# Block attention and two expert networks: scores of two heads in one visit on 64 rows each, late jobs staggered by one, products of the second network in another order

## Chip, cores and metric

The kernel runs on one core of a Trainium2 chip. The metric is the device time of one execution in microseconds (us); smaller is better. The time before is 913.89 us, the median of three runs (913.84 to 914.25).

## What is computed

Four sequences of 576 tokens go through attention with 8 heads of 64, with a mask by blocks of 64 tokens (a query sees its own block of keys and all earlier ones). The result, 2304 tokens by 512, goes through a network that takes the larger of three products, and then through a gated network:

```python
scores = scale * np.matmul(q, k.transpose(0, 1, 3, 2))      # (4, 8, 576, 576)
scores = np.where(block_i >= block_j, scores, -1e9)
attn = softmax(scores)
x = np.matmul(attn, v)                                       # then (2304, 512)
h = np.maximum(np.maximum(x @ w1, x @ w2), x @ w3)           # 512 -> 768
x = h @ w_out                                                # 768 -> 512
gate = 1.0 / (1.0 + np.exp(-(x @ w_gate)))                   # 512 -> 1536
out = (gate * (x @ w_val)) @ w_out2                          # 1536 -> 512
```

## The kernel before

The first part holds attention and the first network ("experts"), the second part the gated network. Most products are made in fp32r, a faster form of fp32 that keeps fewer bits; so an operand is split into a high part (rounded) and a low part (what is left), and a product becomes three: high by high, high by low, low by high. Value products and transposes stay in fp32.

**Jobs.** Attention is cut into 32 jobs. A job is a sequence and a pair of heads. Sixteen early jobs take the first 256 queries and keys (row blocks 0 and 1 of 128 queries), sixteen late jobs the other 320 queries (row blocks 2 and 3, and the 64 queries of block 4) with all 576 keys. A job loads keys, queries and values (`load_qk`, `load_v`), splits keys and queries (`high_q` and a copy make the high parts, `low_q` and a subtraction the low ones), and makes scores (`scores`, lines 383 and 384). Masking (`hide`), the largest score, the exponential with its sum (line 405) and the division (`norm`) follow on VectorE and ScalarE. The weights are transposed on TensorE (`turn`, line 458; block 4 in `turn_four`, line 474) and copied to the tile `PT` (`keep`, `keep_four`); `apply` (line 496) multiplies them by the values, one head on columns 0 to 63 of the array and one on 64 to 127. `split` then writes the high and low parts of the result for the experts.

**Scores before.** The queries' tile holds high parts in rows 0 to 63 and low parts in rows 64 to 127, the keys stand twice, once for each half. So two matmuls over 128 rows make all of one head's scores for a row block:

```python
T.matmul(s, j.qp[:, qc : qc + 128], KP[:, h, ck], start=True, stop=False)   # 383
T.matmul(s, j.qp[:, qc : qc + 128], KL[:, h, ck], start=False, stop=True)   # 384
```

Block 4 has 64 queries of each head. Both heads' queries stand side by side with zeros between, four matmuls of 288 columns for each half of the keys (`scores_four`, lines 425 and 426).

**Experts.** Chunks of 256 tokens (early) and 320 (late) go through `experts` (lines 529 to 531, twelve matmuls a step) and `project` (lines 574 to 576).

**Order.** TensorE has two streams: A is attention, M the experts. A table `visits` places the steps of attention (S0, S1 and S4 are scores, T0, T1 and T4 transposes, P the value products) between expert steps, with lengths `LEN`; numbers in `PLAN` set starts, gaps and due times. `plan` then goes through all operations in time, with a cost for each, and decides which engine's instruction comes next; every engine issues in that order, SP's DMAs as well. Besides, the weights of the gated network, which arrive in a 64-bit format, are converted, combined and parked in DRAM during the first part.

**Second part.** The gated network takes blocks of 768 tokens as two by two halves and makes four products of halves from seven (Winograd's form of Strassen's method). `product` issues one of the seven as six matmuls of 384 columns (lines 1207 to 1209), in three banks a, b and c for each of its twelve blocks of weights: 1 and 2 go to a, 6, 7 and 4 to b, 5 and 3 to c. `first`, `last` and `middle` set the order 1 6 5, then 3 and 4 of the previous one (written 3' 4'), then 2 7. Additions on VectorE (line 1220) and a copy on ScalarE (line 1291) read a bank before the next product adds into it. `take_w` loads weights, `out_unit` (lines 1261 to 1263) makes the output.

Of the kernel before, what the change touches and what calls it, by code (L numbers as in the profile page):

```python
# [8 lines left out]
F32 = mybir.dt.float32  # L9
# [25 lines left out]
QKN = 2 * S + 640  # L35
# [12 lines left out]
    "t0": 7.09,  # L48
    "gap0": 0.34,
    "wgap": -0.02,  # L50
    "tail": 3,
    "prep": 2.18,
    "soft": 4.73,
    "keep": 2.54,
    "xsplit": 4.81,
    "evac": 1.08,
    "hcast": 5.75,
    "convb": 50.0,
    "load": 22.63,
    "park0": 116.98,  # L60
    "park": 19.23,
    "parko": 8.0,
    "slack": 100.0,
    "spare": 0.29,
    "start": 79.92,
# [5 lines left out]
RING = {"qk": 2, "v": 4, "s": 3, "t": 2, "o": 1, "m": 2, "w": 8, "raw": 4, "tmp": 4, "st": 3}  # L71
# [3 lines left out]
def block_attention_moe_moe(ctx: ExitStack, tc, k1, q1, v1, k2, q2, vt, wa, wb, out):  # L75
# [55 lines left out]
    ps_o = att.enter_context(tc.tile_pool(name="ps_o", bufs=RING["o"], space=PSUM))  # L131

    ident = ap1.tile([128, 128], F32, name="ident")
    zero = ap1.tile([128, 64], F32, name="zero")
# [3 lines left out]
    QP = [ap1.tile([128, 704], F32R, name=f"Q{i}") for i in range(2)]  # L138
    KP = ap1.tile([128, 2, S], F32R, name="K")
    KL = ap1.tile([128, 2, S], F32R, name="L")  # L140
# [5 lines left out]
    PT = ap1.tile([128, 2, 1408], F32, name="PT")  # L146
    EO = [0, 128, 0, 384]
    SEG = {(0, 2): 0, (0, 3): 1, (1, 2): 2, (1, 3): 3, (2, 2): 4, (2, 3): 5, (3, 3): 6}
# [161 lines left out]
    def add_job(b, p, late):  # L310
        j = Job()
        j.b, j.p, j.late = b, p, late
        j.i = len(jobs)
        j.tiles = (2, 3) if late else (0, 1)
        alt = not late and p % 2
        j.k0 = 288 if alt else 0
        j.nkc = S if late else 256
        j.nq = 320 if late else 256
        j.eo = 448 if alt else 0
        j.qp = QP[j.i % 2]  # L320
        j.qt = [0, 448] if late else [0, 256]
        jobs.append(j)
# [9 lines left out]
    def load_qk(j):  # L332
        n = 2 * j.nkc
        if j.i < 3:

            j.raw = first[:, 1024 * j.i : 1024 * j.i + 1024]
# [15 lines left out]
    def kcols(j, n=None):  # L352
        return slice(j.k0, j.k0 + (n or j.nkc))

    def high_q(j):
        if j.late:
            for h in range(2):
                A.activation(j.qp[0:64, 384 * h : 384 * h + 320], j.qr[:, h], AF.Copy, scale=SCALE)
        else:
            A.activation(j.qp[0:64, :512], j.qr.rearrange("p h n -> p (h n)"), AF.Copy, scale=SCALE)  # L360

    def low_q(j):
        def f(o, i, hi):
            V.scalar_tensor_tensor(out=o, in0=i, scalar=SCALE, in1=f32(hi), op0=ALU.mult, op1=ALU.subtract)

        if j.late:
            for h in range(2):
                c = slice(384 * h, 384 * h + 320)
                f(j.qp[64:128, c], j.qr[:, h], j.qp[0:64, c])
        else:  # L370
            f(j.qp[64:128, :512], j.qr.rearrange("p h n -> p (h n)"), j.qp[0:64, :512])

    def scores(j, h, i):

        ps = ps_s.tile([128, 512], F32, tag="s", name="ps_s")
        j.bank[h, i] = ps
        ts = (j.tiles[i],) if j.late else j.tiles
        for t in ts:
            s = ps[:, : 128 * (t + 1)] if j.late else ps[:, 128 * t : 128 * t + 128 * (t + 1)]
            j.s[h, t] = s  # L380
            qc = j.qt[h] + 128 * (t - j.tiles[0])
            ck = kcols(j, 128 * (t + 1))
            T.matmul(s, j.qp[:, qc : qc + 128], KP[:, h, ck], start=True, stop=False)  # L383
            T.matmul(s, j.qp[:, qc : qc + 128], KL[:, h, ck], start=False, stop=True)  # L384

# [12 lines left out]
    def largest_score(j, h, i):  # L398
        c = 2 * h + i
        V.tensor_reduce(out=j.nm[:, c : c + 1], in_=j.s[h, j.tiles[i]], axis=AX.X, op=ALU.max, negate=True)  # L400

    def expo(j, h, i):
        t, c = j.tiles[i], 2 * h + i
# [11 lines left out]
    def norm(j, h, i, e):  # L415
        t, c = j.tiles[i], 2 * h + i
# [3 lines left out]
    def scores_four(j, i):  # L420
# [40 lines left out]
    def keep(j, h, g, e):  # L461
        ps, n = j.tp[h, g[0]], len(g)
        if j.late:
            o = 192 * SEG[g[0]]
            d = PT[:, h, o : o + 192 * n].rearrange("p (s c) -> p s c", c=192)[:, :, :128]
            copy(e, d, ps[:, : 128 * n].rearrange("p (s c) -> p s c", c=128))
# [10 lines left out]
    def keep_four(j, i, e):  # L477
        if i == 0:
            d = PT[:, :, :1152].rearrange("p h (k s) -> p k h s", k=3)[:, :, :, 128:192]
            copy(e, d, j.tp4[0][:, 0:3])  # L480
        elif i == 1:
            copy(e, PT[:, :, 192 * 5 + 128 : 192 * 6], j.tp4[0][:, 3])
        else:
            copy(e, PT[0:64, :, 192 * 6 + 128 : 192 * 7], j.tp4[1][0:64, 0])

    def apply(j):


        j.o = ps_o.tile([128, 512], F32, tag="o", name="ps_o")
        if j.late:  # L490
            parts = [(0, 0, 320), (384, 0, 320), (768, 0, 320), (1088, 128, 192), (1280, 128, 64)]
# [133 lines left out]
    for j in jobs:  # L625
        p = jobs[j.i - 1] if j.i else None
        if not j.late:
            visits += [[(j, "S0"), (j, "S1")], [(p, "T0"), (p, "T1")] if p else [], [(p, "P")] if p else []]
        else:
            v = [[(j, "S0")], [(j, "S4")], [(j, "S1")], [(j, "T0")], [(j, "T4")], [(j, "T1")]]  # L630
            v[1].append((p, "P"))
            if not p.late:
                v[0] = [(p, "T0"), (p, "T1")] + v[0]
            visits += v
    visits += [[], [(jobs[-1], "P")]]
    LEN = {"S0": (0.47, 0.82), "S1": (0.47, 0.82), "S4": (0, 1.06), "T0": (0.35, 0.77),
           "T1": (0.35, 0.77), "T4": (0, 0.5), "P": (0.95, 2.5)}
# [41 lines left out]
    def build():  # L679
        z = Op("V", 0.6, lambda: (V.memset(zero, 0.0), V.memset(PT[64:128, :, 1280:1344], 0.0)), [])  # L680
# [176 lines left out]
        def job(j):  # L857
# [3 lines left out]
            ring = "qk" if i >= 3 else None  # L861
            ld = Op("S", 0.2, lambda: load_qk(j), [], ring=ring, size=384e3 if not j.late else 752e3)
            lv = Op("S", 0.1, lambda: load_v(j), [], ring="v", size=128e3 if not j.late else 320e3)
            kold = after(*[S_ops[x] for x in range(max(0, i - 2), i) if x in S_ops and (j.late or x == i - 2)])
            qold = S_ops.get(i - 2, [])
            n = j.nkc * 2
            kh = Op(*both(n, False), lambda e: copy(e, KP[:, :, kcols(j)], j.kr), [ld] + kold)
            zq = []
            if j.late and i < 4 * B + 2:
                zq = [Op("V", 0.15, lambda: V.tensor_copy(j.qp[:, 320:384], zero), qold + [z])]  # L870
            qh = Op("A", 0.56 if not j.late else 0.8, lambda: high_q(j), [ld] + qold)
            kl = Op(*vec(n), lambda: sub("V", KL[:, :, kcols(j)], j.kr, f32(KP[:, :, kcols(j)])), [kh])
            ql = Op("V", 0.61 if not j.late else 0.84, lambda: low_q(j), [qh])
# [3 lines left out]
            prep = [kl, ql] + zq  # L877
# [3 lines left out]
            N = {0: [], 1: []}  # L881
            eold = [j2 for j2 in (jobs[i - back],)] if i >= back else []
# [3 lines left out]
            Tn = {}  # L886
            RC = []

            def softmax(h, s, k, head):
# [3 lines left out]
                x = Op(*act(n, 1), lambda: expo(j, h, k), after([r], *[e.t_ops[h] for e in eold]))  # L893
                r.late = x.late = pos(f"S{h}") + P["soft"]
                s.frees.append(x)
                X[h].append(x)

            for h in range(2):
                for k in range(2) if j.late else (0,):
                    c = (0.36, 0.465)[k] if j.late else 0.46  # L900
                    s = pe("A", c, lambda h=h, k=k: scores(j, h, k), prep, pos(f"S{h}") + 0.1 * k, ring="s")
                    S_ops[i].append(s)
                    d = [s]
                    hd = Op("V", 0.11 if j.late else 0.13, lambda h=h, k=k: (small(j) if h == 0 and k == 0 else None, hide(j, h, k)), d + ([first_hide] if (h, k) != (0, 0) else []))
                    if (h, k) == (0, 0):
                        first_hide = hd
                    hd.late = pos(f"S{h}") + P["soft"]
                    for kk in ((k,) if j.late else (0, 1)):
                        softmax(h, s, kk, hd)
                if j.late and h == 0:  # L910
# [494 lines left out]
```

## Time and profile before

| | |
|---|---|
| median of three runs | 913.89 us |
| the profiled execution's own time | 915.82 us |
| its span | 914.0 us |
| TensorE busy | 887.0 us (97%) |
| VectorE busy | 597.8 us (65%) |
| ScalarE busy | 487.5 us (53%) |
| chain of waits, TensorE's share | 86% |
| granted TensorE clock over the span | 0.996 |

A busy share is an average over the whole span, and the engines have different shares in different stages; so the windows by stage are needed beside it. Matmuls overlap each other, so the distance from one start to the next tells what one costs, and not its duration. A record of the trace may be half of an instruction: value products are ten instructions with 320, 192 and 64 columns and twenty records.

### The profile page before, as it was taken

What the parts mean: (1) busy time and instruction counts of PE and PEld (TensorE: products, weight loads), DVE (VectorE), ACT (ScalarE), POOL (GpSimd) and SP (SyncE); (2) the same over time, 40 slices, a digit from 0 to 9 for tenths busy, and PEclk for the clock granted to TensorE, in tenths of its full rate; (3) what the DMA queues carried; (4) which work ended last, traced back from release to release, by engine and by line L of the source; (5) the groups of instructions that cost most, each with busy time, mean ns of one, the idle gap of its engine ahead of it and who ended that gap; (6) DMA issues with size and microseconds to landing.
All of it is one profiled execution on the core that took longest, in us unless ns stands there. A gap on an engine that the chain in (4) does not pass through costs nothing.

```text
span 914.0 us, 15702 instructions
## 1 busy us (share of the span) xinstructions
PE 887.0 (97%) x5696; PEld 826.0 (90%) x5696; DVE 597.8 (65%) x1372; ACT 487.5 (53%) x1098; POOL 96.6 (11%) x91
## 2 busy tenths in 40 slices
PE   5799999999999999999999998999999999999997
PEld 4689999999989989998999898888999988999986
DVE  7999958789899799788643876851455630455400
ACT  6889435457567566467422664631666621566311
POOL 0000000000000000000001553400132300132300
PEclk9899999999999999999999999999999999999999
DMA  9942345524655645643534988863789743779232
GB/s 314 374 121 63 99 143 174 182 75 154 209 165 191 199 148 174 189 137 104 188 119 143 310 249 259 279 213 132 247 251 320 238 130 129 251 259 310 78 104 80
DMA packets 85885, 171.42 MB, mean 188 GB/s; under 512 B 11312, under 2 KB 24624, under 8 KB 85808
## 3 DMA queue, kind: packets, MB, share of 16 engines
q1 hardware_dynamic: 85808, 170.43, 57.5%
q8 instruction: 44, 0.72, 0.3%
q14 instruction: 33, 0.27, 0.1%
HBM read 132.64 MB, written 37.75 MB: 186 GB/s over the span
## 4 chain that ended last, share of the span: by engine, by line
PE 86%; DVE 7%; DMA 3%; ACT 2%; issue 1%; SPq 0%; ACTq 0%; DVEq 0%
PE acc L1207 8%; PE acc L1209 8%; PE acc L1208 8%; PE ps_m L529 8%; PE ps_m L531 7%; PE ps_m L530 7%; PE acc L1262 5%; PE acc L1263 5%; PE acc L1261 5%; PE ps_o L496 5%; PE ps_t L458 3%; PE ps_m L574 3%; PE ps_m L576 3%; PE ps_m L575 3%; PE ps_s L383 2%; PE ps_s L384 2%
## 5 line engine op out<-in xcount | busy, mean ns | idle before, releaser
L529 PE MATMUL ps_m<-XT,w 128*128 128x256 f32 (+1 forms) x576 | 176.0, 305 | 1.6 <-ACT m L538 0.6
L530 PE MATMUL ps_m<-XT,w 128*128 128x256 f32 (+1 forms) x576 | 170.4, 296 | 0.8 <-DVE XT L98 0.8
L531 PE MATMUL ps_m<-XT,w 128*128 128x256 f32 (+1 forms) x576 | 170.6, 296 | 0.4 <-DVE w L98 0.3
L529 PEld LDWEIGHTS ps_m<-XT,w 128*128 128x128 f32 x576 | 109.0, 189 | 5.3 <-ACT m L538 1.1
L530 PEld LDWEIGHTS ps_m<-XT,w 128*128 128x128 f32 x576 | 109.2, 190 | 1.9 <-DVE XT L98 1.0
L531 PEld LDWEIGHTS ps_m<-XT,w 128*128 128x128 f32 x576 | 109.0, 189 | 0.8 <-DVE w L98 0.8
L1262 PE MATMUL acc<-ow,hid 128*128 128x512 f32 x216 | 84.2, 390 | 0.0
L1263 PE MATMUL acc<-ow,hid 128*128 128x512 f32 x216 | 84.2, 390 | 0.0
L1261 PE MATMUL acc<-ow,hid 128*128 128x512 f32 x216 | 84.0, 389 | 0.0
L405 ACT ACTIVATE E<-ps_s,nm 128x256 f32<-128x256 f32 (+3 forms) x128 | 66.5, 526 | 21.5 <-DVE nm L400 20.2
L1209 PE MATMUL acc<-xc,wgx 128*128 128x384 f32 x216 | 72.2, 334 | 0.0
L1207 PE MATMUL acc<-xc,wgx 128*128 128x384 f32 x216 | 72.2, 334 | 0.0
L1208 PE MATMUL acc<-xc,wgx 128*128 128x384 f32 x216 | 72.2, 334 | 0.0
L1220 DVE TENSOR_TENSOR u<-acc,p 128x384 f32<-128x384 f32 x72 | 40.0, 556 | 42.3 <-PE acc L1209 40.0
L93 DVE COPY osb<-acc 128x512 f32<-128x512 f32 x6 | 4.2, 692 | 95.3 <-PE acc L1263 88.8
L1220 DVE TENSOR_TENSOR u<-acc,u 128x384 f32<-128x384 f32 x72 | 40.0, 556 | 38.4 <-PE acc L1209 37.2
L1175 ACT CAST ow<-or 128x512 fp32r<-128x512 f32 x36 | 22.4, 621 | 74.0 <-PE acc L1263 55.8
L400 DVE TENSOR_REDUCE nm<-ps_s 128x1 f32<-128x256 f32 (+3 forms) x128 | 56.7, 471 | 1.5 <-ACT E L405 0.2
L540 DVE TENSOR_TENSOR m<-ps_m,m 128x256 f32<-128x256 f32 (+1 forms) x96 | 43.6, 454 | 20.9 <-PE ps_m L531 19.3
L496 PE MATMUL ps_o<-PT,v 128*64 128x320 f32 (+3 forms) x448 | 53.7, 374 | 3.6 <-issue 1.8
L574 PE MATMUL ps_m<-HR,w 128*128 128x320 f32 (+1 forms) x184 | 55.4, 301 | 0.0
L576 PE MATMUL ps_m<-HR,w 128*128 128x320 f32 (+1 forms) x184 | 54.6, 297 | 0.0
(135 smaller groups left out, 2217.9 us busy)
## 6 DMA issues: line engine op xcount, KB each, us to landing
praw<-in_wb_dram SPq DMA_DIRECT2D x36, 512.0 KB, 4.1
wr<-pairs SPq DMA_DIRECT2D x72, 256.0 KB, 3.6
wr<-pairs SPq DMA_DIRECT2D x36, 384.0 KB, 4.1
qk<-in_k_dram SPq DMA_DIRECT2D x16, 576.0 KB, 4.2
or<-outs SPq DMA_DIRECT2D x36, 256.0 KB, 3.5
wgx<-lowp SPq DMA_DIRECT2D x24, 384.0 KB, 3.7
wland<-in_wa_dram SPq DMA_DIRECT2D x5, 1536.0 KB, 17.1
wgz<-lowp SPq DMA_DIRECT2D x24, 256.0 KB, 4.1
```

The source lines that it names most:

```text
L496: T.matmul(j.o[rows(h), d : d + n], j.v[:, h, k, :], PT[:, h, c : c + n], start=(k == 0), stop=(k == len(parts) - 1), skip_group_check=True,)
L529: T.matmul(ps, wt[:, 0, w, k], xh[:, k], start=(k == 0), stop=False)
L530: T.matmul(ps, wt[:, 0, w, k], xl[:, k], start=False, stop=False)
L531: T.matmul(ps, wt[:, 1, w, k], xh[:, k], start=False, stop=(k == KD - 1))
L574: T.matmul(ps, wh, hh, start=(f == 0), stop=False)
L576: T.matmul(ps, wl, hh, start=False, stop=(f == NF1 - 1))
L1207: T.matmul(ps, w[:, 0, h], x[:, 0, h], start=start and h == 0, stop=False, skip_group_check=True)
L1208: T.matmul(ps, w[:, 0, h], x[:, 1, h], start=False, stop=False, skip_group_check=True)
L1209: T.matmul(ps, w[:, 1, h], x[:, 0, h], start=False, stop=h == 1, skip_group_check=True)
L1261: T.matmul(ps, h[:, 0, ct], w[:, 0], start=(f == 0), stop=False)
L1262: T.matmul(ps, h[:, 0, ct], w[:, 1], start=False, stop=False)
L1263: T.matmul(ps, h[:, 1, ct], w[:, 0], start=False, stop=(f == NF2 - 1))
```

## The change

- Keys are loaded once and not doubled, in one DMA with the queries. The tile of a job's queries has a high and a low half beside each other, and so have its keys; head 0 stands in rows 0 to 63, head 1 in rows 64 to 127.
- `scores` makes a row block of both heads: three products (high by high, high by low, low by high) for each head, on 64 rows, the heads in turn, into two banks. The product of low by low parts, which the two matmuls had in them, is left out. `scores_four` takes 128 rows with three matmuls for each half of the keys, from queries that the host lays out with zeros.
- Visits: S0 and S1 of the next late job stand behind P of the last one, S4 of the next job behind T4 of this one. T0 transposes row block 2 of both heads (six), T1 row block 3 (eight); before, T0 was one head and T1 the other.
- Banks: four for scores and two for transposes and value products; before three, two and one.
- Block 4's transposes are copied with two copies where there were three.
- The second part's order is 1 6 5 4' 2 3' 7.
- Numbers in `PLAN` and `LEN` change with it, among them the starts of the parking (`park0` 116.98 to 125) and of the first visits.

```diff
-        j.kr = j.raw[:, :n].rearrange("p (h n) -> p h n", h=2)
-        j.qr = j.raw[0:64, n : n + 2 * j.nq].rearrange("p (h n) -> p h n", h=2)
-        nc.sync.dma_start(out=j.raw[:, :n], in_=(k2 if j.late else k1)[j.b, j.p])
-        nc.sync.dma_start(out=j.raw[0:64, n : n + 2 * j.nq], in_=(q2 if j.late else q1)[j.b, j.p])
+        n = j.nkc + j.nq
+        j.kr, j.qr = j.raw[:, : j.nkc], j.raw[:, j.nkc : n]
+        nc.sync.dma_start(out=j.raw[:, :n], in_=(kq2 if j.late else kq1)[j.b, j.p])
...
-    def scores(j, h, i):
-
+    PARTS = ((0, 0), (0, 1), (1, 0))
+
+    def bank_s(j, h, i):
         ps = ps_s.tile([128, 512], F32, tag="s", name="ps_s")
         j.bank[h, i] = ps
...
+    def scores(j, i):
+
+        bank_s(j, 1, i)
+        for t in (j.tiles[i],) if j.late else j.tiles:
+            q0 = 128 * (t - j.tiles[0])
+            for n, (a, b) in enumerate(PARTS):
+                for h in range(2):
+                    T.matmul(
+                        j.s[h, t], j.qp[rows(h), a, q0 : q0 + 128], j.kp[rows(h), b, : 128 * (t + 1)],
+                        start=(n == 0), stop=(n == 2),
+                    )
...
-        for h, q in ((0, j.qp[:, 256:384]), (1, j.qp[:, 320:448])):
-            T.matmul(s, q, KP[:, h, c], start=(h == 0), stop=False)
-            T.matmul(s, q, KL[:, h, c], start=False, stop=(h == 1))
+        for n, (a, b) in enumerate(PARTS):
+            T.matmul(s, j.qp[:, a, 256:384], j.kp[:, b, c], start=(n == 0), stop=(n == 2))
...
-        j.o = ps_o.tile([128, 512], F32, tag="o", name="ps_o")
+        j.o = ps_t.tile([128, 512], F32, tag="t", name="ps_o")
...
-            v = [[(j, "S0")], [(j, "S4")], [(j, "S1")], [(j, "T0")], [(j, "T4")], [(j, "T1")]]
-            v[1].append((p, "P"))
...
+    for j, p, x in zip(later, [None] + later, later[1:] + [None]):
+        visits += [
+            ([(p, "P")] if p else []) + ([(x, "S0"), (x, "S1")] if x else []),
+            [(j, "T0")],
+            [(j, "T4")] + ([(x, "S4")] if x else []),
+            [(j, "T1")],
+        ]
...
             t = first(n, t)
             if n:
-                t = last(n - 1, t)
-            t = middle(n, t)
+                t = fourth(n - 1, t)
+            t = second(n, t)
+            if n:
+                t = third(n - 1, t)
+            t = seventh(n, t)
```

How the instructions move is seen in the built programs' order. First TensorE, about the value products of a late job, before (`K` and `L` are high and low keys, `Q` queries, `ps_s` scores, `PT` transposed weights, `ps_m` expert products):

```order
1405 L576 MATMUL ps_m<-HR,w 128x256
1406 L425 MATMUL ps_s_3214<-K,Q_151 128x288
1407 L426 MATMUL ps_s_3214<-L,Q_151 128x288
1408 L425 MATMUL ps_s_3214<-K,Q_151 128x288
1409 L426 MATMUL ps_s_3214<-L,Q_151 128x288
1410 L496 MATMUL ps_o<-PT,v 64x320 x6
1411 L496 MATMUL ps_o<-PT,v 64x192 x2
1412 L496 MATMUL ps_o<-PT,v 64x64 x2
1413 L574 MATMUL ps_m<-HR,w 128x256
```

And the same place in the changed program (`K_149` and `Q_147` hold both parts now, `E` is the tile of exponentials):

```order
1180 L516 MATMUL ps_m<-XT,w 128x256
1181 L481 MATMUL ps_o<-PT,v 64x320 x6
1182 L481 MATMUL ps_o<-PT,v 64x192 x2
1183 L481 MATMUL ps_o<-PT,v 64x64 x2
1184 L369 MATMUL ps_s<-K_149,Q_147 128x384 x6
1185 L369 MATMUL ps_s<-K_149,Q_147 128x512 x6
1186 L445 MATMUL ps_t<-ident,E_151 128x128 x3
1187 L445 MATMUL ps_t<-ident,E_152 128x128 x3
1188 L514 MATMUL ps_m<-XT,w 128x256
```

Block 4's scores have left this visit, the twelve score matmuls of the next job have come, and here the transposes of T0 follow at once; in later slots one or two expert steps of twelve matmuls stand between.

Second, VectorE near the start, before, about the preparation of the fifth job (`qk` is the loaded tile, `wraw` a weight being converted):

```order
20 L95 TENSOR_SCALAR E_156<-E_156,rc 128x256
21 L93 CAST K<-qk 128x2x256
22 L364 SCALAR_TENSOR_TENSOR Q_152<-qk,Q_152 64x512
23 L93 COPY PT<-ps_t 128x384
24 L98 TENSOR_TENSOR L<-qk,K 128x2x256
25 L714 TENSOR_SCALAR wraw<-wraw 128x512
```

And in the changed program:

```order
34 L349 SCALAR_TENSOR_TENSOR Q_147<-qk,Q_147 128x256
35 L94 COPY PT<-ps_t 128x384
36 L99 TENSOR_TENSOR w<-wraw,w 128x512
37 L94 CAST K_149<-qk 128x256
38 L701 TENSOR_SCALAR wraw<-wraw 128x512
39 L400 TENSOR_SCALAR rc<-sm 128x4
40 L401 RECIPROCAL rc<-rc 128x4
41 L99 TENSOR_TENSOR K_149<-qk,K_149 128x256
```

The copy and the two subtractions of a job are 256 wide instead of 512, and other work stands between them.

## Rows read from the trace of the kernel before

**Rows 1.** Page, busy us (share of the span) xinstructions.

```profile
PE 887.0 (97%) x5696; PEld 826.0 (90%) x5696; DVE 597.8 (65%) x1372; ACT 487.5 (53%) x1098; POOL 96.6 (11%) x91
```

**Rows 2.** Windows by stage: length, busy per engine, granted clock, DMA share, GB/s.

```profile
0.00:33.00 33.00, 21.17 (x94) 15.30 (x95) 25.19 (x79) 22.77 (x67) 0.70 (x6) 0.90 0.96 343
33.00:81.00 48.00, 43.85 (x348) 39.76 (x344) 47.20 (x130) 44.07 (x122) 0.00 (x0) 1.00 0.53 167
81.00:178.00 97.00, 97.00 (x808) 93.22 (x808) 77.13 (x211) 47.91 (x136) 0.00 (x0) 1.00 0.46 143
178.00:490.00 312.00, 311.50 (x2277) 291.75 (x2276) 250.72 (x639) 182.28 (x429) 3.10 (x2) 1.00 0.47 152
490.00:580.00 90.00, 84.11 (x481) 82.47 (x481) 66.39 (x101) 46.27 (x89) 36.89 (x30) 1.00 0.84 271
580.00:914.00 334.00, 329.35 (x1699) 303.51 (x1697) 131.20 (x217) 144.16 (x258) 55.92 (x53) 1.00 0.61 198
```

**Rows 3.** Timeline of TensorE, one head's late scores: start, duration, instruction.

```profile
311.40 0.34 PE L383 MATMUL ps_s<-K,Q 128*128 128x384 f32 x1
...
312.21 0.31 PE L529 MATMUL ps_m<-XT,w 128*128 128x320 f32 x1
```

**Rows 4.** Timeline of TensorE, block 4's scores and the value products.

```profile
301.44 0.29 PE L425 MATMUL ps_s<-K,Q 128*128 128x288 f32 x1
...
301.84 0.29 PE L426 MATMUL ps_s<-L,Q 128*128 128x288 f32 x1
302.06 2.27 PE L496 MATMUL ps_o<-PT,v 128*64 128x320 f32 x20
304.26 0.41 PE L574 MATMUL ps_m<-HR,w 128*128 128x320 f32 x1
304.51 0.31 PE L575 MATMUL ps_m<-HR,w 128*128 128x320 f32 x1
304.66 0.31 PE L576 MATMUL ps_m<-HR,w 128*128 128x320 f32 x1
```

**Rows 5.** Timeline of TensorE, seven transposes.

```profile
313.98 0.93 PE L458 MATMUL ps_t<-ident,E 128*128 128x128 f32 x7
314.66 0.39 PE L529 MATMUL ps_m<-XT,w 128*128 128x320 f32 x1
```

**Rows 6.** Timeline of TensorE, value products of rows 4, two, four, six records.

```profile
302.06 0.49 PE L496 MATMUL ps_o<-PT,v 128*64 128x320 f32 x2
...
302.06 0.76 PE L496 MATMUL ps_o<-PT,v 128*64 128x320 f32 x4
...
302.06 1.03 PE L496 MATMUL ps_o<-PT,v 128*64 128x320 f32 x6
```

**Rows 7.** Timeline of TensorE, early scores of the second head.

```profile
105.25 0.22 PE L383 MATMUL ps_s<-K,Q 128*128 128x128 f32 x1
105.31 0.27 PE L384 MATMUL ps_s<-L,Q 128*128 128x128 f32 x1
...
105.71 0.82 PE L458 MATMUL ps_t<-ident,E 128*128 128x128 f32 x6
```

**Rows 8.** Groups of VectorE from 0 to 33 us: count, busy, mean ns, idle before.

```profile
L364 DVE SCALAR_TENSOR_TENSOR Q<-qkv,Q 64x512 fp32r<-64x512 f32 x3 | 2.1, 685 | 1.8 <-ACT Q L360 1.7
...
L98 DVE TENSOR_TENSOR L<-qkv,K 128x512 fp32r<-128x512 f32 x3 | 2.1, 684 | 0.1
...
L98 DVE TENSOR_TENSOR XT<-ps_o,XT 128x256 fp32r<-128x256 f32 x3 | 1.3, 420 | 0.0
```

**Rows 9.** Waits: us in total, times, longest us.

```profile
PE acc L1207 <- DVE u L1220: 5.8, 4, 1.9
```

**Rows 10.** Timeline of VectorE and TensorE at the longest of those waits.

```profile
516.60 0.55 DVE L1220 TENSOR_TENSOR u<-acc,p 128x384 f32<-128x384 f32 x1
517.18 0.56 DVE L1220 TENSOR_TENSOR u<-acc,u 128x384 f32<-128x384 f32 x1
...
517.89 0.41 PE L1207 MATMUL acc<-xc,wgy 128*128 128x384 f32 x1 [1.92 <-DVE u L1220]
```

More of the change, by code (lines that the diff above doesn't have):

```diff
@@ L47 @@
 PLAN = {
[L48 to L57, printed above, removed]
+    "t0": 5.89,
+    "gap0": 1.98,
+    "wgap": -0.06,
+    "tail": 4,
+    "prep": 1.73,
+    "soft": 4.55,
+    "keep": 5.8,
+    "xsplit": 4.79,
+    "evac": 1.93,
+    "hcast": 5.66,
     "convb": 50.0,
     "load": 22.63,
-    "park0": 116.98,
-    "park": 19.23,
+    "park0": 125,
+    "park": 18.72,
     "parko": 8.0,
     "slack": 100.0,
-    "spare": 0.29,
-    "start": 79.92,
+    "spare": 0.3,
+    "start": 120,
     "pair": 4,
@@ L624, in block_attention_moe_moe @@
     visits = []
[L625 to L629, printed above, removed]
-            v = [[(j, "S0")], [(j, "S4")], [(j, "S1")], [(j, "T0")], [(j, "T4")], [(j, "T1")]]
-            v[1].append((p, "P"))
[L632 to L637, printed above, removed]
+    early, later = jobs[: 4 * B], jobs[4 * B :]
+    for j, p in zip(early, [None] + early):
+        visits += [[(j, "S0")], [(p, "T0"), (p, "T1")] if p else [], [(p, "P")] if p else []]
+    p = early[-1]
+    visits += [[(p, "T0"), (p, "T1")], [(p, "P"), (later[0], "S0"), (later[0], "S1")], [(later[0], "S4")]]
+    for j, p, x in zip(later, [None] + later, later[1:] + [None]):
[5 more added lines that the diff above has]
+        ]
+    visits.append([(later[-1], "P")])
+    LEN = {"S0": (0.97, 0.75), "S1": (0, 0.92), "S4": (0, 0.8), "T0": (0.35, 0.7),
+           "T1": (0.35, 0.92), "T4": (0, 0.5), "P": (0.95, 2.5)}
     place = {}
@@ L860, in job @@
             back = 1 if j.late else 2
-            ring = "qk" if i >= 3 else None
-            ld = Op("S", 0.2, lambda: load_qk(j), [], ring=ring, size=384e3 if not j.late else 752e3)
+            ring = "qk" if i >= NF else None
+            ld = Op("S", 0.2, lambda: load_qk(j), [], ring=ring, size=262e3 if not j.late else 492e3)
             lv = Op("S", 0.1, lambda: load_v(j), [], ring="v", size=128e3 if not j.late else 320e3)
[L864 to L873, printed above, removed]
+            old = S_ops.get(i - 2, [])
+            n = j.nkc
+            kh = Op(*both(n, False), lambda e: copy(e, j.kp[:, 0, : j.nkc], j.kr), [ld] + old)
+            qh = Op(*act(j.nq), lambda: high_q(j), [ld] + old)
+            kl = Op(*vec(n), lambda: sub("V", j.kp[:, 1, : j.nkc], j.kr, f32(j.kp[:, 0, : j.nkc])), [kh])
+            ql = Op(*vec(j.nq), lambda: low_q(j), [qh])
             ld.frees = [kl, ql]
@@ L880, in job @@
             X = {0: [], 1: []}
-            N = {0: [], 1: []}
-            eold = [j2 for j2 in (jobs[i - back],)] if i >= back else []
+            eold = [jobs[i - back]] if i >= back else []
             if j.late and i == 4 * B:
                 eold = jobs[i - 2 : i]
-            Tn = {}
-            RC = []
             def softmax(h, s, k, head):
@@ L892, in softmax @@
                 r = Op(*vec(n), lambda: largest_score(j, h, k), [head])
-                x = Op(*act(n, 1), lambda: expo(j, h, k), after([r], *[e.t_ops[h] for e in eold]))
-                r.late = x.late = pos(f"S{h}") + P["soft"]
+                x = Op(*act(n, 1), lambda: expo(j, h, k), after([r], *[e.t_ops[h, k] for e in eold]))
+                r.late = x.late = pos(f"S{k if j.late else 0}") + P["soft"]
                 s.frees.append(x)
[L896 to L907, printed above, removed]
+                X[k].append(x)
@@ new lines, in first_bank @@
+            def first_bank(j, k):
+                if k == 0:
+                    small(j)
+                bank_s(j, 0, k)
+            for k in range(2) if j.late else (0,):
+                c = (0.75, 0.92)[k] if j.late else 0.97
+                s0 = pe("A", 0.0, lambda k=k: first_bank(j, k), prep, pos(f"S{k}"), ring="s")
+                s1 = pe("A", c, lambda k=k: scores(j, k), prep, pos(f"S{k}") + 0.01, ring="s")
+                S_ops[i] += [s0, s1]
+                for h, s in enumerate((s0, s1)):
+                    hd = Op("V", 0.11 if j.late else 0.13, lambda h=h, k=k: hide(j, h, k), [s1])
+                    hd.late = pos(f"S{k}") + P["soft"]
@@ L961, in job @@
             turns(1)
-            p = pe("A", 0.95 if not j.late else 2.5, lambda: apply(j), keeps + [lv], pos("P"), ring="o")
+            p = pe("A", 0.95 if not j.late else 2.5, lambda: apply(j), keeps + [lv] + ([z] if i == 4 * B else []), pos("P"), ring="t")
             P_ops[i] = [p]
@@ L1295, in first, with second @@
             return t
-        def middle(n, t):
+        def second(n, t):
             on(t, product(c, n, 1, "a", False))
@@ L1307, in middle, with fourth, third @@
             return t
-        def last(n, t):
+        def fourth(n, t):
+            on(t, product(c, n, 3, "b", False))
+            t += PD
+            on(t, add(c, n, "p1", "b", "p1"))
+            finish(c, n, 1, 0, "p1", t + 0.6)
+            return t
+        def third(n, t):
             on(t, product(c, n, 2, "c", False))
@@ L1332, in block_attention_moe_moe @@
                 if f == 0 and i == 3:
-                    t = last(NF2 - 1, t)
+                    t = third(NF2 - 1, fourth(NF2 - 1, t))
                     if c + 1 < TOK // HC:
```

145 lines of the change are left out of this document (60 added, 85 removed).

## The prediction

> **What bounds the kernel now.** I read the page's busy shares first: TensorE has 887.0 us of work in a span of 914.0 [rows 1]. Then the windows by stage [rows 2]. From 81 to 178 us TensorE has no idle time at all, and from 178 to 490 only 0.5 us: there the time is the sum of what stands in TensorE's queue, and an instruction taken out of that queue is worth its issue time. Before 81 us TensorE is short of work (21.17 of 33 us, then 43.85 of 48), while VectorE is at 47.20 of 48 and the DMA engines at a share of 0.96 in the first 33 us: there the feeders count. The second network's first block (490 to 580) idles 5.9 us; the rest of it has none but the 4.65 us behind the last product. So the change has four places, and each has another price. Prices are start-to-start distances from the timeline, since the durations of matmuls overlap.
>
> **Late scores (178 to 490 us, sixteen jobs).** Before, one head takes four matmuls over all 128 rows (384, 384, 512, 512 columns), 0.81 us from the first to the next work [rows 3], both heads 1.62. The change issues twelve matmuls of 64 rows, in six pairs, one head on each half of the rows. If a pair costs what one full matmul of its width costs, that is three quarters: 1.215 us, 0.405 less. The fifth row block's scores go from eight matmuls of 0.133 us ((301.84 − 301.44) / 3) [rows 4] to six over all rows: 1.06 to 0.80, 0.27 less.
>
> Whether a pair costs one or two is the disputed price, since no 64-row matmul stands in the trace of before. The nearest rows are the value products, which use half of the columns each: two, four and six records end at 0.49, 0.76 and 1.03 us after the same start [rows 6], so a pair of 320 columns takes 0.27 us, 0.84 ns a column. One transpose, also fp32 but over all columns, takes (314.66 − 313.98) / 7 = 0.097 us for 128 [rows 5], 0.76 ns a column. The pair costs about what one would: halves overlap. Bounds are 1.0 and 2.0 times a single matmul; I take 1.0, by these rows, for rows as for columns.
>
> Changing from whole to half columns also costs: the value products start 0.22 us after the last score, which alone takes 0.133, so 0.09; and the first matmul behind them takes 0.25 us where the next takes 0.15 [rows 4], so 0.10. Before, a job has that pair of changes once (value products). Now it goes value products, scores, whole array: one change more, 0.10 us. Bounds for it are 0 and 0.3. The sixteen jobs give 16 × (0.405 + 0.27 − 0.10) = **9.2 us**. The transposes stay fourteen per job, in two visits with a change behind each, as before: nothing.
>
> The Trainium skill (TensorEngine Tiling (Array Packing), Key Properties) states that a change of tiling mode, not just of the tile, drains TensorE. For column halves the trace agrees (the 0.09 and 0.10 us); for row halves no run here shows it yet. By that rule the extra 0.10 us belongs in the sum; without it the sum would be 1.6 us larger.
>
> **Early scores (81 to 178 us, seven jobs).** One head takes 105.71 − 105.25 = 0.46 us for four matmuls of 128 and 256 columns, both 0.92; the shortest distance is 0.06 us [rows 7]. Now there are twelve with a weight load each. If each needs at least the 0.06, that is 0.72, and one more change makes 0.82; if pairs run at half of 0.115 it is 0.79; one after the other 1.48. I take no gain: small matmuls are where loads cost most. Range over seven: −2.5 to +1 us if halves overlap.
>
> **The start (0 to 81 us).** A job's keys are no longer doubled: 128 KB of 384 KB go, one DMA issue of two, and VectorE's two subtractions fall from 512 to 256 columns, 0.685 to about 0.42 each (the subtraction of 256 columns in the same stretch) [rows 8]. That is 0.53 us a job, with the narrower key copy some 0.7. Five jobs are prepared in the first 33 us: 3.5 us of VectorE, on a chain that ends in the first expert matmul. Six more come by 81 us, where TensorE still idles 4.1 us. But the weights' DMAs fill the engines, and the bytes saved (0.65 MB at the 343 GB/s of that row) are only 1.9 us. So the gain lies between 0 (weights decide) and 7 us; I take **3.5**, nearest to the VectorE rows, because VectorE is full on both sides of 33 us. The granted clock there is 0.90 [rows 2]; what it does after the change is part of the same bounds.
>
> **The second network's order.** Four waits of TensorE for a VectorE addition cost 5.8 us, the longest 1.9 [rows 9]. In that one, TensorE resumes at 517.89, behind the second of two additions, which ends at 517.74; the first ended at 517.15 [rows 10]. The old order comes to product 3 third behind 7, and product 3 adds into the bank that the second addition reads. The new one has 4 in that place, whose bank the first addition reads; 3 comes two products later. So each wait shrinks by about 0.57 us: **2.3 us**. The price is product 2, now three products behind 1 instead of four, so a copy by ScalarE has 1.04 us less to clear the bank. Bounds: all 5.8 gone, or one wait of 1.9 added.
>
> **Sum.** 9.2 + 0 + 3.5 + 2.3 = 15.0 us. The profiled execution took 915.82 (span 914.0 and 1.8 around it), 1.9 above the median of the three runs, 913.89; so 900.8 on its own footing, and **899 us** as a median. About 0.2%, 1.8 us, is what a measurement of this kernel can tell from no change.
>
> **Costed at nothing, with what hides it.** Of the value products only the buffer is new: they take one of the two transposition banks, and the next transposes wait for VectorE's subtraction (about 0.42 to 0.49 us) a step later; if VectorE were late, the transposes would be late next. The scores move up by one job: their banks (now four) are held until the previous job's transposes have freed the exponentials' buffers, and loads go out one slot earlier on SP; with DMA at a share of 0.47 from 178 to 490 [rows 2] that has room. On SP each job issues one key and query DMA where it issued two, so nothing is pushed back. The weight parking on SP and POOL keeps its own times.
>
> **Rivals.**
> - *Halves take turns.* The twelve matmuls of a late job then cost 12 × 0.2025 = 2.43 us against 1.62: 0.81 more, less the 0.27, plus 0.10, makes 16 × 0.64 = 10.2 lost; early 7 × (1.48 − 0.92) = 3.9 lost; the 5.8 of start and second network stays. Sum +8.3: **922 us**, slower. Against it stands [rows 6]; for it, that those are columns and these rows. It decides once a pair costs 1.8 times a single (late jobs alone break even at 1.47).
> - *Halves overlap in part.* At 1.25 times a single the scores take 1.52, the gain per job is 0.27 and the sum is 15.0 − 4.9 = 10.1: **904 us**. The Trainium skill (TensorE: Matmul & The Clock Gate, Measured speedup vs the span model) gives 3.07 for four tiles of 32 rows, not 4, which would be a factor of 1.3; an estimate by that page is 905 us. No run here shows it.
> - *A wait takes the place of the visit.* The value products now follow the last transposes after one expert step of twelve matmuls, 12 × 0.15 = 1.8 us [rows 4], where scores stood between as well. Two copies of 512 columns come out of those transposes; by 0.42 us for 256 columns [rows 8] one takes up to 0.84, and both on VectorE 1.7. With one more subtraction of about 0.7 ahead of them, each visit would wait 0.6 us: 16 × 0.6 = 9.6 lost, **908 us**. Against it: from 178 to 490 us TensorE hardly ever waited [rows 2], ScalarE can take one of the copies, and both engines get less to do there.
> - *The gain is not there*, because the planner's new order hands it back at the start or between the networks: within 2 us of 914.
>
> **How the numbers follow.** The forecast has 0.72; overlap in part 0.10; the new wait 0.06; halves in turns 0.08; no gain 0.04. Within the forecast the bounds give 15.0 + 2.5 + 3.5 + 3.5 = 24.5 us (889) at best. At worst, with the switch at 0.3 and a pair at 1.1, late jobs give 4.1, the early ones lose 1, the start gives nothing and the second network loses 1.9: 1.2 us (913). The range, with the corners cut and both faster rivals inside, is 890 to 911. Faster by over 0.2%: 0.72 + 0.10 + half of the new wait + 0.01 of the rest = 0.86. Within: 0.05. Slower: 0.09.
>
> **What would show it.** Right: the two records of a score pair start some hundredths of a us apart and the next pair about 0.18 (384 columns) or 0.23 us (512) behind; value products and scores in one visit of about 3.6 us; TensorE without idle time from 90 to 480 us; the second network starting some 13 us sooner; its first block idling under 4 us. Wrong: pairs at 0.35 or 0.45 us; TensorE waiting for a copy out of the transposes before the value products; an end of the first part no earlier than 485 us.

## The result, and the profile after

The changed kernel takes 904.36 us (median of four runs, 903.46 to 906.56) where the kernel before took 914.07 on the same chip: a ratio of 0.9886, 95% interval 0.985 to 0.9922, 9.7 us less. In the two profiled executions it is 903.46 against 915.82, 12.4 less: the one of before lay 1.75 us above its median, the one of after 0.9 below. A second series of the changed kernel (below) gave 905.31 and 0.9896.

The page's busy times and the windows by stage, after:

```profile
PE 876.6 (97%) x5792; PEld 810.4 (90%) x5792; DVE 581.0 (64%) x1369; ACT 455.8 (51%) x1050; POOL 96.3 (11%) x91
```

```profile
0.00:33.00 33.00, 21.55 (x138) 15.19 (x139) 26.93 (x98) 25.45 (x78) 0.70 (x6) 0.90 0.94 351
33.00:81.00 48.00, 45.31 (x390) 41.02 (x389) 44.72 (x130) 41.82 (x118) 0.00 (x0) 1.00 0.41 140
81.00:178.00 97.00, 97.00 (x831) 91.62 (x830) 65.07 (x190) 51.35 (x152) 0.00 (x0) 1.00 0.42 140
178.00:430.00 252.00, 252.00 (x1943) 229.41 (x1942) 217.32 (x591) 128.82 (x330) 0.00 (x0) 1.00 0.40 131
430.00:476.00 46.00, 42.02 (x283) 41.23 (x282) 26.45 (x46) 14.85 (x27) 0.00 (x0) 1.00 0.53 177
476.00:566.00 90.00, 88.12 (x515) 87.17 (x514) 64.09 (x101) 49.19 (x93) 39.27 (x32) 1.00 0.84 280
```

Against [rows 1, 2]: TensorE has 10.4 us less to do; it still never waits from 81 to 430 us; VectorE is less full up to 81 us (44.72 of 48 us where it had 47.20). New is the window from 430 to 476 us, where TensorE idles 4.0 us. In the last window, 1.9 us of idle time stand where [rows 2] had 5.9.

The timeline of TensorE in one late job: the last expert matmul ahead, value products, scores, and block 4's scores (three dots stand for rows between):

```profile
314.47 0.31 PE L516 MATMUL ps_m<-XT,w 128*128 128x320 f32 x1
314.71 2.28 PE L481 MATMUL ps_o<-PT,v 128*64 128x320 f32 x20
...
316.92 0.44 PE L369 MATMUL ps_s<-K,Q 64*128 64x384 f32 x2
...
317.20 0.51 PE L369 MATMUL ps_s<-K,Q 64*128 64x384 f32 x4
...
317.37 0.57 PE L369 MATMUL ps_s<-K,Q 64*128 64x384 f32 x4
...
317.55 0.63 PE L369 MATMUL ps_s<-K,Q 64*128 64x512 f32 x4
...
318.01 0.40 PE L369 MATMUL ps_s<-K,Q 64*128 64x512 f32 x2
318.34 0.41 PE L514 MATMUL ps_m<-XT,w 128*128 128x320 f32 x1
318.59 0.31 PE L515 MATMUL ps_m<-XT,w 128*128 128x320 f32 x1
318.74 0.31 PE L516 MATMUL ps_m<-XT,w 128*128 128x320 f32 x1
...
323.08 1.04 PE L413 MATMUL ps_s<-K,Q 128*128 128x288 f32 x6
323.96 0.31 PE L514 MATMUL ps_m<-XT,w 128*128 128x320 f32 x1
```

A row that begins at a pair (x4: with the next pair) shows where that pair starts: 0.17 us apart for 384 columns, 0.23 for 512; the two records of a pair start 4 ns apart. The first pair takes 0.28, the last 0.33 to the next work, and the first matmul behind takes 0.25 where the next takes 0.15. Twelve matmuls cost 318.34 − 316.92 = 1.42 us, block 4's six 0.88. The expert matmul ahead of the value products takes 314.71 − 314.47 = 0.24 where others take 0.15.

The new waits, in TensorE's timeline, and what ScalarE and SP's queue do there:

```profile
439.77 0.41 PE L514 MATMUL ps_m<-XT,w 128*128 128x320 f32 x1 [0.51 <-ACT m L523]
...
446.39 0.41 PE L514 MATMUL ps_m<-XT,w 128*128 128x320 f32 x1 [1.07 <-DVE m L525]
...
456.10 0.42 PE L514 MATMUL ps_m<-XT,w 128*128 128x320 f32 x1 [2.40 <-ACT m L523]
```

```profile
446.74 0.42 ACT L523 COPY m<-ps_m 128x320 f32<-128x320 f32 x1
454.71 0.67 ACT L737 ACTIVATE praw<-praw 128x512 f32<-128x512 f32 x1 [7.55 <-DMA praw<-in_wb_dram]
455.28 0.45 ACT L543 CAST HR<-m 128x320 fp32r<-128x320 f32 x1
455.62 0.42 ACT L523 COPY m<-ps_m 128x320 f32<-128x320 f32 x1
```

```profile
445.40 0.53 SPq L1080 DMA_DIRECT2D xraw<-x2d  x1
446.03 0.56 SPq L773 DMA_DIRECT2D outs<-outw  x1
446.64 0.43 SPq L123 DMA_DIRECT2D praw<-in_wb_dram  x1
...
467.44 0.37 SPq L123 DMA_DIRECT2D praw<-in_wb_dram  x1
```

ScalarE stands 7.55 us at weights of the parking (`praw`), whose load was issued 1.2 us behind the second load of the second part's x (`xraw`); the copy `m` that empties an expert bank stands behind in ScalarE's queue, and TensorE waits for it. Four loads of the parking stand behind that load of x, the last at 467.44 us. Before, the parking's last load stood ahead of it:

```profile
444.15 0.38 SPq L122 DMA_DIRECT2D praw<-in_wb_dram  x1
...
460.11 0.56 SPq L1095 DMA_DIRECT2D xraw<-x2d  x1
```

### The profile page after: what moved, and what is told of

The parts are those of the page before. It is cut to its first block, busy times and chain, and to the rows that moved or that the text cites. A ratio compares the mean times of both kernels' runs of the same rounds, so it can differ in the third digit from the quotient of the medians.

```text
span 901.6 us, 15860 instructions
## 1 busy us (share of the span) xinstructions
PE 876.6 (97%) x5792; PEld 810.4 (90%) x5792; DVE 581.0 (64%) x1369; ACT 455.8 (51%) x1050; POOL 96.3 (11%) x91
## 4 chain that ended last, share of the span: by engine, by line
PE 44%; DMA 3%; DVE 1%; ACT 1%; issue 1%; POOL 1%; SPq 0%; ACTq 0%; DVEq 0%; POOLq 0%
PE acc L1192 8%; PE acc L1193 8%; PE acc L1194 8%; PE acc L1248 5%; PE acc L1247 5%; PE acc L1246 5%; DMA wr<-pairs 1%; DMA praw<-in_wb_dram 1%; PE ps_m L514 1%; PE ps_m L516 1%; DMA or<-outs 1%; PE ps_m L515 1%; POOL wgz L99 0%; DVE u L1205 0%; ACT wgx L1131 0%
## 5 line engine op out<-in xcount | busy, mean ns | idle before, releaser
L388 DVE TENSOR_REDUCE nm<-ps_s 128x1 f32<-128x256 f32 (+3 forms) x128 | 54.4, 470 | 2.8 <-ACT E L393 2.8
L559 PE MATMUL ps_m<-HR,w 128*128 128x320 f32 (+1 forms) x184 | 55.6, 302 | 0.0
L561 PE MATMUL ps_m<-HR,w 128*128 128x320 f32 (+1 forms) x184 | 54.5, 296 | 0.0
L560 PE MATMUL ps_m<-HR,w 128*128 128x320 f32 (+1 forms) x184 | 54.5, 296 | 0.0
```

The costliest lines, as they stand in the source:

```text
L559: T.matmul(ps, wh, hh, start=(f == 0), stop=False)
```

## Experiments

Before, run beside them, had medians of 915.05, 914.73 and 915.08 us in the three series; ratios are to it.

**The order of products alone, and taken back.** E1 is the kernel before with `first`, `fourth`, `second`, `third`, `seventh`; E2 the changed kernel with the old functions:

```diff
-                t = fourth(n - 1, t)
-            t = second(n, t)
-            if n:
-                t = third(n - 1, t)
-            t = seventh(n, t)
+                t = last(n - 1, t)
+            t = middle(n, t)
```

> The kernel before, with the second part's products in the new order 1 6 5 4' 2 3' 7 and nothing else changed. The step of the prediction (each of the four waits for an addition shrinks by about 0.57 us) gives 2.3 us less than before, about 911.7. My theory after the traces (a product that adds into a bank now comes late enough behind the addition that the wait goes altogether) gives 4.5 to 5.5 us less, about 909, with under 1.5 us of TensorE waiting for the additions. The rival, that the waits went for another reason (the second part starts earlier and beside other transfers), gives no change, within 1 us of before.

> The changed kernel with the products in the old order 1 6 5 3' 4' 2 7. My theory: the waits for the additions come back, 4 to 5.5 us more than the changed kernel's 904.4, about 909; the first part's end (485.2 us in the trace of the changed kernel) stays. The step of the prediction gives 2.3 more, 906.7. The rival (another reason for the waits) gives 904.4 within 1 us.

E1: 911.76 us, ratio 0.9963 (0.9949 to 0.9976), 3.3 less. E2: 908.26, ratio 0.9923 (0.9903 to 0.9942), 2.9 more than the changed kernel's 905.31 of a later series and 2.6 more than E4's 905.70 of its own, which is as fast as the changed kernel. TensorE's waits for the additions, first in E1 (where [rows 9] had 5.8), then in the changed kernel, then in E2:

```profile
PE acc L1207 <- DVE u L1220: 1.2, 2, 0.7
```

```profile
PE acc L1192 <- DVE u L1205: 1.2, 2, 0.7
```

```profile
PE acc L1192 <- DVE u L1205: 3.8, 4, 1.4
```

The order is what shortens the waits. It doesn't always take them away: the other traces with the new order have 1.2 to 2.9 us of them (2.8 in E12). It is worth about 3 us, between the prediction's step and my theory, which took the 5.8 us of one execution as typical; E1's interval, 2.2 to 4.7 us, reaches both 2.3 and 4.5.

**The parking 8 us sooner.** E3:

```diff
-    "park0": 125,
+    "park0": 116.98,
```

> The changed kernel with the parking of the weights started by the plan at 116.98 us, as before, where the change has 125. My theory: the last loads of the parking are then through before the load of the second part's x goes out, ScalarE is not held 7.55 us at the parked weights, and the waits of TensorE for the copies m (0.51 and 2.40 us, and 1.07 for VectorE's) go: 3 to 4 us less than the changed kernel's 904.4, about 901. The rival (these waits come from the staggered late jobs, whose work on ScalarE and VectorE stands closer together) gives 904.4 within 1 us, with the same waits around 440 to 456 us.

906.37 us, ratio 0.9899 (0.9876 to 0.9921): no gain. Two loads of the parking stand behind the second load of x instead of four, the first of them still 1.2 us behind it (445.56 and 446.80 us), and the wait is 2.60 us. This edit didn't test the theory.

**Three matmuls on one half, then three on the other.** E4:

```diff
-            for n, (a, b) in enumerate(PARTS):
-                for h in range(2):
+            for h in range(2):
+                for n, (a, b) in enumerate(PARTS):
```

> The changed kernel with the two loops in the score function exchanged, so that three matmuls on the upper half of the rows are followed by three on the lower half, instead of one on each in turn. My theory (neighbouring matmuls run beside each other because they are on opposite halves; matmuls on the same half go one after the other): of a late job's twelve matmuls only those at the three changes of half still overlap; the visit's scores go from 1.2 us to 1.8 at least and 2.4 at most, 16 times 0.6 to 1.2 more, with the early jobs 2 to 4 on top: 12 to 23 us more than the changed kernel's 904.4, 916 to 927. The rival (a 64-row matmul simply costs half of a 128-row one, whatever stands next to it) gives 904.4 within 1 us.

905.70 us, ratio 0.9895 (0.9875 to 0.9916): as the changed kernel. Here my theory fell. The trace still shows six pairs, their records 10 ns apart instead of 4, and twelve matmuls in 1.43 us:

```profile
316.78 0.45 PE L369 MATMUL ps_s<-K,Q 64*128 64x384 f32 x2
...
317.24 0.57 PE L369 MATMUL ps_s<-K,Q 64*128 64x384 f32 x4
...
318.21 0.41 PE L514 MATMUL ps_m<-XT,w 128*128 128x320 f32 x1
```

So either a 64-row matmul simply takes half the time, or the second half's matmuls begin ahead of earlier ones of the first half. The next run tells these apart.

**One head a visit.** E5 (block 4's scores stand behind T1; besides, a score function makes one head, and the operations behind follow their head):

```diff
...
-            ([(p, "P")] if p else []) + ([(x, "S0"), (x, "S1")] if x else []),
-            [(j, "T0")],
-            [(j, "T4")] + ([(x, "S4")] if x else []),
-            [(j, "T1")],
+            ([(p, "P")] if p else []) + ([(x, "S0")] if x else []),
+            [(x, "S1")] if x else [],
+            [(j, "T0")],
+            [(j, "T4")],
+            [(j, "T1")] + ([(x, "S4")] if x else []),
...
```

> The changed kernel with a late job's scores cut by head instead of by row block: the six matmuls of head 0 (all on the upper 64 rows) in one visit, the six of head 1 (lower 64 rows) in a visit of their own, expert matmuls of 128 rows between; the fifth block's scores stand behind the second transposes. No matmul on the other half can run beside them. Theory one, the halves really overlap: a 64-row matmul alone takes as long as a pair, 0.17 us (384 columns) and 0.23 (512), each visit about 1.2 us, together 2.4 where both heads took 1.2 in the changed kernel; with two more changes of mode at 0.2, 16 times 1.6 = 26 us more, about 930. Theory two, a 64-row matmul simply takes half the time: a matmul every 0.085 and 0.115 us, only the changes of mode are added, 16 times 0.4 = 6 us more, about 911.

918.66 us, ratio 1.0035 (1.0018 to 1.0052), 13 more than the changed kernel. A job's two visits, six matmuls alone on the upper half and, 12 us later, six alone on the lower, and then a job whose two visits the planner put next to each other:

```profile
301.30 0.44 PE L379 MATMUL ps_s<-K,Q 64*128 64x384 f32 x1
...
301.58 0.75 PE L379 MATMUL ps_s<-K,Q 64*128 64x384 f32 x3
...
302.72 0.41 PE L569 MATMUL ps_m<-HR,w 128*128 128x320 f32 x1
```

```profile
313.04 0.44 PE L379 MATMUL ps_s<-K,Q 64*128 64x384 f32 x1
...
314.46 0.33 PE L455 MATMUL ps_t<-ident,E 128*128 128x128 f32 x1
...
343.82 0.44 PE L379 MATMUL ps_s<-K,Q 64*128 64x384 f32 x1
...
345.69 0.42 PE L524 MATMUL ps_m<-XT,w 128*128 128x320 f32 x1
```

Six alone take 1.42 us (302.72 − 301.30; 314.46 − 313.04), as long as the twelve in pairs. So a lone 64-row matmul costs what a pair costs, and the halves do run beside each other. Six of one and six of the other half in a row take 1.87: a half runs ahead of the other by three matmuls without loss (E4), by six not quite. Nine of the sixteen jobs had separate visits (+1.42 each), seven adjacent ones (+0.45): 15.9 us, less about 2.5 for waits at the first part's end, 1.7 here where the changed kernel has 4.0 to 4.3; the expected 26 had all sixteen separate, at 1.6 each.

**The parking ahead of the load of x.** E6:

```diff
-    "park0": 125,
-    "park": 18.72,
+    "park0": 118,
+    "park": 14.5,
```

> The changed kernel with the parking planned from 118 us in steps of 14.5 us instead of from 125 in steps of 18.72 (the earlier run showed that 116.98 alone moves the last loads by one place only and leaves one behind the load of x). Now the last load of weights to be parked stands ahead of the second load of x on SP. My theory: ScalarE is not held some 7.5 us for parked weights at 447 us, the waits of TensorE at 446 and 456 us (1.07 to 1.67 and 2.3 to 2.6) go, and with them the stretch from 456 to 466 us at a granted clock of 0.83 to 0.85 that three of the runs showed: 3 to 5 us less than the changed kernel, 900 to 902 where that takes 904.4 to 905.7. Rival one: these waits come from the late jobs and stay, no change within 1 us. Rival two: the parking, now denser between 118 and 340 us, holds VectorE and ScalarE there and TensorE waits in that stretch, 2 us or more slower.

902.16 us, ratio 0.9866 (0.9842 to 0.9889). No load of the parking stands behind the second load of x, ScalarE's 7.5 us are gone and so is the wait at 456. Waits for `m` of 0.80 and 1.78 us near 440 and 448 remain in this execution, where the expectation had the one near 446 go too. A wait of 2.2 to 2.7 us near 456 us stands in every trace in which parked loads come behind the second load of x (the changed kernel, E2, E3, E4, E9, E10), and in none of the other traces of the new kernel (E5 to E8, E11, E12).

**No stagger, and the old numbers.** E7 scores a late job directly ahead of its own transposes (this loop in place of the one over the late jobs); E8 has the whole old table `PLAN`:

```diff
...
+    for j, p in zip(later, [p] + later):
+        visits += [[(p, "P"), (j, "S0"), (j, "S1")], [(j, "S4")], [(j, "T0")], [(j, "T4")], [(j, "T1")]]
```

> The changed kernel with the late jobs not staggered: a late job's row blocks 2 and 3 are scored behind the value products of the job before, then block 4's scores, then its three visits of transposes, five visits a job where the change has four and scores the next job already between the transposes of this one. TensorE's work is the same, with the same changes of mode. If the stagger is what lets TensorE go on without a wait, the transposes wait for the exponentials and divisions, 0.5 to 1.5 us a job, 8 to 24 us more than the changed kernel. My expectation: the five visits leave about 7 us between scores and transposes, which is about what masking, largest score, exponential and division take, so waits of 0 to 0.3 us a job, 0 to 5 us more, 905 to 910.

> The changed kernel with the whole table of planner numbers of before (first visits at 7.09 us with a gap of 0.34, due times, parking from 116.98 in steps of 19.23). Theory one, the start is faster because a job has half of the keys to load and split: the 48th expert step starts within 2 us of the changed kernel's (some 6 us ahead of before), the time stays within 2 us of the changed kernel. Theory two, the new numbers made the start faster: it falls back by about 4 us, to 908 to 909. On the parking's numbers: the steps of 19.23 leave as many loads behind the load of x, so the waits at 440 to 456 us stay.

E7: 903.11 us, ratio 0.9873 (0.985 to 0.9897): no slower, where 905 to 910 was expected. Its windows:

```profile
178.00:430.00 252.00, 250.12 (x1904) 226.81 (x1903) 206.32 (x578) 138.58 (x344) 0.00 (x0) 1.00 0.43 140
430.00:476.00 46.00, 45.47 (x313) 43.89 (x312) 25.22 (x45) 16.50 (x30) 0.25 (x1) 1.00 0.44 151
```

It waits 1.9 us where the staggered kernel waits for nothing, and 0.5 where that waits 4.0. So with these numbers the stagger costs about what it saves. Part of its cost is the collision with the parking: the numbers are those of the changed kernel and the first part ends at the same 485.1 us, but the second load of x goes out at 461.23 us and not at 445.40, behind the whole parking:

```profile
440.04 0.43 SPq L123 DMA_DIRECT2D praw<-in_wb_dram  x1
...
461.23 0.53 SPq L1075 DMA_DIRECT2D xraw<-x2d  x1
```

E8: 906.29, ratio 0.9903 (0.9876 to 0.9931). The next matmul after 900 of the experts starts at 179.6 us; 182.1 before, 177.8 after: theory one holds for the time, but with the old numbers only 2.5 of the 4.3 us gained by there are left. The granted clock of the first 33 us was 0.79 in this execution, 0.90 in the two others, so the split isn't settled. The expectation on the parking missed: with the old numbers its last load (450.43 us) stands ahead of the second load of x (455.30 us), and of the three waits one of 1.9 us is left, for VectorE, near 450 us. So the new numbers and the stagger together make the collision.

**The last series.** E9 is the changed kernel again, E11 the one without stagger with the parking of E6. E10 and E12 add to the changed kernel and to E6 this:

```diff
-            take_x(c, TB - 27.0)
+            take_x(c, TB - 17.0)
```

> The changed kernel once more, as it is, beside the three that follow, so that they are compared on the same chip. Expected: 904 to 906 us, the waits of 0.5, 1.07 and 2.4 us at 440, 446 and 456 us again.

> The changed kernel with the preparation of the second part's x (differences, high and low parts, on VectorE and ScalarE) planned 10 us later, at 17 us ahead of the planned end of the first part instead of 27; the parking stays as it is. Theory one, TensorE's waits near 440 to 456 us come from ScalarE held for parked weights alone: they stay, no change within 1 us of the changed kernel. Theory two, both the preparation of x and the parked weights stand ahead of the copies and maxima m in the queues of ScalarE and VectorE there: without the preparation in that stretch the wait at 446 us for VectorE goes (1.07) and the one at 456 shrinks or goes, 1 to 4 us less than the changed kernel.

> The kernel without the stagger and with the parking from 118 us in steps of 14.5: the whole parking then stands ahead of the first load of x on SP. Expected: no wait of TensorE over 0.5 us between 430 and 476 us; about 1.9 us of waits between 178 and 430 us as without the stagger alone; 1 to 3 us less than the changed kernel, about 902. If the denser parking holds VectorE in the stretch where the unstaggered jobs wait for it, up to 3 us more than that.

> The changed kernel with both: the parking from 118 us in steps of 14.5 and the preparation of x at 17 us ahead of the planned end. If the two causes add, no wait of TensorE over 0.5 us is left between 178 us and the end of the first part, which comes 4 us sooner than in the changed kernel, at about 481 us: about 900 to 901 where that takes 904 to 905. If moving the preparation later makes the second part wait for x instead, that shows as a wait of TensorE at the second part's start and gives back what is gained.

The number 17 moves no instruction on any engine (the built programs have the same order), so E10 is a repetition of the changed kernel and E12 one of E6, and what the preparation of x does stays open. Read so, E9 and E10 gave 905.31 and 905.12 us (0.9896 and 0.9888), E12 902.58 (0.9861, 0.9839 to 0.9884), E11 903.59 (0.9867, 0.9846 to 0.9888), no gain over E7 where about 902 was expected; E12 was expected at 900 to 901. The parking ahead of x thus gives 2.6 us in one series, where three of E12's four executions are faster than all eight of E9 and E10; E6's version is the fastest here, 1.3 to 1.4% below the kernel before. The waits in the trace of E9, then of E12, and the windows behind them in E9, E10 and E12:

```profile
PE ps_m L514 <- ACT m L523: 3.3, 2, 2.7
PE ps_m L514 <- DVE m L525: 1.1, 1, 1.1
```

```profile
PE ps_m L514 <- DVE m L525: 1.1, 1, 1.1
PE ps_m L514 <- ACT m L523: 0.5, 1, 0.5
```

```profile
456.00:466.00 10.00, 9.21 (x52) 9.21 (x53) 4.44 (x9) 2.32 (x6) 0.00 (x0) 0.83 0.48 158
```

```profile
456.00:466.00 10.00, 10.00 (x60) 10.00 (x59) 3.91 (x8) 2.45 (x6) 0.00 (x0) 0.83 0.46 150
```

```profile
456.00:466.00 10.00, 10.00 (x70) 10.00 (x69) 2.66 (x6) 1.78 (x4) 0.00 (x0) 1.00 0.11 42
```

Behind a wait of over 2 us the granted clock of these 10 us fell to 0.83 in E9 and E10, a third of them at the lower level, 1.2 GHz; E10 got 60 matmuls through where E12 got 70, and 10 of 0.147 us are 1.5 us. The changed kernel's first profile kept 1.00 behind the same wait, so its runs may differ by about that.

## Why the prediction was right, and where its terms were off

The direction held, and 904.4 us lies in the range; the number itself, 899, was 5.4 too low. Term by term, in the profiled executions:

- **Late scores: 9.2 predicted, 7.7 measured** (start-to-start distances of the scores of all sixteen jobs, 27.7 to 23.0 us and 18.4 to 14.0 for block 4, less 1.4: the change to the value products took 0.09 from block 4's last score before [rows 4] and takes it from the expert matmul ahead now, 0.24 for 0.15). The disputed price came out as taken: a pair costs what one matmul costs, and E5 shows that it is overlap. Mis-sized was the one change of mode more, charged with 0.10 us a job. The twelve took 1.42 and not 1.215, with 0.10 lost at either end, so it cost 0.20, and the 0.10 that was not charged, sixteen times, is the difference; the slow first expert matmul (0.25) is no loss, since before it stood behind the value products. The Trainium skill (TensorEngine Tiling (Array Packing), Key Properties) says that a change of mode drains TensorE; the trace agrees for row halves, with these numbers.
- **Early scores: 0 predicted**, 0.89 us against 0.93 a visit, 0.3 in all. **Start: 3.5 predicted, 3.3 to 4.3 measured** (4.3 by the matmul after 900 of the experts, early scores among them; 3.3 is what the first part's 7.3 us and its new waits, 4.0, leave beside the 7.7 and 0.3). By E8 some half of it may hang on the planner's numbers and not on the subtractions it was derived from, and the granted clock of the first 33 us differs from trace to trace of the new kernel, from 0.79 to 1.00: its cause isn't shown.
- **Second network: 2.3 predicted, about 3 by E1 and E2**; 5.1 between the two profiles, where the 5.8 us of before were at the high end. The mechanism was right: product 3 two places later. Its size went by one pair of additions.
- **What was left out: 4.0 us of waits ahead of the second part**, and up to 1.5 of clock. The step that failed is "the weight parking on SP and POOL keeps its own times": its last load went from 444.2 to 467.4 us, and the second load of x, which no term had, from 460.1 to 445.4, so that four parked loads stand behind it where there was none. The first part, which ended 7.3 us sooner (485.20 against 492.47), doesn't explain this alone, since E7 ends it as early without the collision. E6 and E12 show that this accounts for 2.6 us; the waits of 0.5 to 1.8 us that remain weren't settled.

The four terms measured come to about 15 us again, because the late scores' shortfall happens to be made up by the others; that is luck. Less the 4.0 us of waits and up to 1.5 of clock it is some 9 to 11 us, and 9.7 was measured.

Of the rivals, halves in turn and overlap in part fell by the 0.17 and 0.23 us; the estimate of 904 for the latter met the time by chance, with another mechanism. No wait for the transposes' copies appeared from 81 to 430 us. Of the signs of being right, the spacing of the pairs, the visit of 3.6 us and the short idle time of the second network's first block came; but TensorE went without idle time to 439 us and not to 480, and the second part started 7 us sooner instead of 13. Its start at 485.2 us is also one of the signs named for being wrong ("no earlier than 485 us"): those were what pointed to the missing 5 us.

## What to carry to other kernels

When an order or a planner's numbers change, list what is timed near the end of the stage, loads above all, and see what is now in the same place: here the gain was cut by loads that the prediction took to stay where they were. Two heads of 64 rows each run beside each other at the price of one, whether the matmuls alternate singly or in threes, but each entry into the mode and each exit has to be paid, so join visits in the same mode. Size a stall by several executions: the waits for the additions were 5.8 and 3.8 us in two traces with the old order, and 1.2 to 2.9 with the new one.

## What was not expected of the hardware

- The two row halves need no alternation in the program: three matmuls on one half ahead of three on the other cost 1.43 us where pairs cost 1.42 (E4), six and six 1.87 where six alone take 1.42 (E5). The Trainium skill (TensorEngine Tiling (Array Packing), Key Properties) says that different tiles can load weights and multiply in parallel, which the trace shows; that one runs three matmuls ahead stands only in these runs.
- A wait of 2.2 to 2.7 us near 456 us was followed by 10 us at a mean granted clock of 0.83 to 0.85 in five executions (E2, E3, E4, E9, E10) and of 1.00 in the changed kernel's first profile, the same program as E9.
